# Two row stores moved from SyncE's DMA queue to GpSimd's, one pace point and one convolution slot moved later, in a fused convolution and gated feed-forward kernel

## The chip, the cores and the metric

The kernel runs on one core of one Trainium2 chip. The metric is the device time of one execution in microseconds; several executions are taken and their median is given. A separate execution is recorded by the hardware profiler, and every time of a single instruction or transfer below comes from that one. The engines are called as the profile calls them: PE is TensorE's matrix multiply and PEld its weight load, DVE is VectorE, ACT is ScalarE, POOL is GpSimd, and SP is SyncE, which here only issues DMAs. SP and POOL each have a DMA queue of their own; both feed the same 16 DMA engines.

## The reference

A depthwise convolution of seven taps (weights put through a softmax, the same for all 24 channels of a head) is followed by a feed-forward layer without a nonlinearity: two products, their elementwise product, and two more products.

```python
w = softmax(weight, axis=-1)                        # 8 heads x 7 taps
out[b, s, h, g] = sum_k w[h, k] * x_pad[b, s + k, h, g]   # x: 8 x 3904 x 192
x = out.reshape(31232, 192)
a = x @ w1                                          # 192 x 1024
b = x @ w2                                          # 192 x 1024
h = a * b @ w3                                      # (a * b) @ w3, 1024 x 1024
return h @ w_out                                    # 1024 x 192, float32
```

## The kernel before

**Tiling.** The tokens are cut into two streams of 15616 (NS = 2), which sit beside each other in the two halves of the partitions. A stream is cut into windows of 58 tokens, and these into 11 blocks, SIZES = 10, 8, 10, 8, then six of 36 and one of 20. A block is what is loaded, convolved and stored at a time. The feed-forward works in rounds of 512 tokens of each stream (31 rounds, taken in groups of four).

**One block's way.** `load_x` (line 98) loads a block's windows of x with DMAs of POOL's queue, which also turn float32 into bfloat16. `conv` (line 262) multiplies each head's windows with a band matrix on PE; the result is copied from PSUM into a `convo` tile by ACT or DVE (line 295). Then it has to be transposed to have channels on the partitions. Blocks 0, 1 and 2 are transposed by PE (`pe_transposes`, line 335). Block 3 onward, and the end of block 2 that round 3 needs, goes through DRAM: `store` (line 300) writes convo to the DRAM tile `rows` with DMAs of SP, and `transposes` (line 343) reads it back with three transposing DMAs of SP for a round, into the ring xT of four rounds. `send` (line 479) issues a round's three transposes as soon as its rows have been stored.

**A round.** `first_product` (line 361) makes both first products, eight steps `ft` of twelve matmuls, ACT copying one result and DVE multiplying it with the other into abT. A round takes 96 matmuls. A dictionary `between` names what is put behind which step: convolutions and PE transposes of the next blocks. `second_product` (line 388) multiplies abT of one stream of one round with W_sb, 32 matmuls, and stores the result; in the first group by POOL, later by SP.

**w3.** W_sb is w3 times w_out, made once. `load_w3` (line 424) copies w3 as bfloat16 to the DRAM tile `w3rows` by two DMAs of POOL, and SP reads it back transposed into w3T with 16 transposing DMAs (`w3_transposes`, line 428): eight for the first 512 rows of w3, eight for the others. `w3_product` (line 433) makes one of eight pieces of W_sb with eight matmuls. Pieces 0 to 3 read what the first eight transposes brought, pieces 4 to 7 the second eight, all eight of them for each piece.

**The order of the work.** The program is scheduled by hand: each engine runs its instructions in the order in which the code issues them and waits only where data or buffers make it. The prologue runs rounds 0 to 3 of first products (lines 484 to 503), with blocks 1 to 3 convolved in between; then the eight w3 products (line 517); then three heads of block 4 (`conv_heads`, line 509, with `slots` 0 to 2 of three, three and two heads, line 515); then the first group's eight second products, with the other heads of block 4 and all of block 5 between them at the places that `at` names (line 534). Behind the last heads of block 4, `conv_heads` stores the part of it that round 4 needs, sends round 4's transposes, and stores the rest; rounds 5 to 7 are sent by the call at line 543.

SP's order around the change is: the first five w3 transposes; six stores, two for the end of block 2 and four for block 3 (lines 494 and 495); the other three w3 transposes of the first half (line 496); round 3's three xT transposes (line 497); the second half's eight w3 transposes (line 498). POOL's order is: the loads of x of blocks 0 to 3 and of the weights; line 500, a copy of two numbers into the tile `pace`, which waits for the ninth w3 transpose since it reads what that one writes; then the ten loads of blocks 4 and 5, which stand behind it; then the zeroing of the padding rows of block 4 (`zero`, line 505), and the eight stores of second products.

Of the kernel before, what the change touches and what calls it, by code (L numbers as in the profile page):

```python
# [16 lines left out]
def kernel(  # L17
# [10 lines left out]
    nc = tc.nc  # L28
# [4 lines left out]
    DFF = moe_w1.shape[1]  # L33
    JT = DFF // 128
# [6 lines left out]
    GROUP = 4  # L41
# [5 lines left out]
    NWIN = (B // NS) * WB  # L47
    LAST = S - (WB - 1) * ST
# [7 lines left out]
    def tok(i):  # L56
        return (i // WB) * S + (i % WB) * ST
# [26 lines left out]
    rows = dram.tile([TS, NP * NS * Q], BF16, name="rows")  # L84
# [51 lines left out]
    pace = const.tile([1, 2], BF16)  # L136
# [31 lines left out]
    for p0 in (0, Q):  # L168
        nc.gpsimd.affine_select(
            out=diag[p0:p0 + Q], in_=ones[p0:p0 + Q].to_broadcast([Q, Q + PAD]),  # L170
# [3 lines left out]
    for r in range(NS):  # L174
        nc.gpsimd.dma_start(out=xb0[Q * r + PAD:Q * r + Q, 0, :],
                            in_=x_rows[r * TS:r * TS + ST, :])
# [13 lines left out]
    def warm(n, t=None):  # L190
# [16 lines left out]
        out=wall, in0=wall, in1=wmax.unsqueeze(2).to_broadcast([1, H, K]), op=ALU.subtract)  # L207
# [6 lines left out]
        out=wrow, in0=wall, in1=wsum.unsqueeze(2).to_broadcast([1, H, K]), op=ALU.mult)  # L214
# [47 lines left out]
    def conv(b, h0, nh, evict=None):  # L262
        n = SIZES[b] // 2
        if h0 == 0:
            convo_of[b] = work.tile([128, n, NP, NS, Q], BF16, tag="convo", bufs=2, name="convo")
        convo = convo_of[b]
        p, cps = banks()
        wd = nh * G

        def view(ps, r):  # L270
            return cps[ps, r, 0:n * wd].rearrange("p (w g) -> p w g", g=wd)

        for j in range(nh):
            h = h0 + j
            for c in range(2):
                xb, w0 = xb_of[b][c]
                for r in range(NS):
                    nc.tensor.matmul(  # L278
                        view(slice(Q * c, Q * c + Q), r)[:, :, j * G:(j + 1) * G],
                        band_of(h, r),  # L280
                        xb[Q * r:Q * r + Q, w0:w0 + n, h * G:(h + 1) * G],
                        start=True, stop=True)
        src = cps[:, :, 0:n * wd].rearrange("p r (w g) -> p r w g", g=wd)
        o, moves = 0, []
        for k, c0, m in segments(h0 * G, wd):
            moves.append((convo[:, :, k, :, c0:c0 + m].rearrange("p w r g -> p r w g"),
                          src[:, :, :, o:o + m]))
            o += m
        if h0 + nh == H:
            del xb_of[b]  # L290
        if evict == ():
            return p, moves
        for e, (dst, part) in enumerate(moves):
            f = evict or [nc.scalar.copy]
            f[e % len(f)](out=dst, in_=part)  # L295
        drained(p)

    stored, sent = [0], [GROUP - 1]

    def store(b, first=0, last=NWIN):  # L300
        n = SIZES[b] // 2
        last = min(last, FIRST[b] + 2 * n)
        stored[0] = tok(last) if last < NWIN else TS
        convo = convo_of[b]
        for c in range(2):
            i0 = FIRST[b] + c * n
            w, end = max(0, first - i0), min(n, last - i0)
            while w < end:
                left = WB - 1 - (i0 + w) % WB
                m = min(end - w, max(1, left))  # L310
                src = convo[Q * c:Q * c + ST, w:w + m].rearrange("s w k r g -> s w (k r g)")
                j0 = tok(i0 + w)
                if left == 0:
                    nc.sync.dma_start(out=rows[j0:j0 + LAST, :], in_=src[0:LAST, 0, :])
                else:
                    dst = rows[j0:j0 + ST * m, :].rearrange("(w s) c -> s w c", s=ST)
                    for s0, s1 in ((0, 48), (48, ST)):
                        nc.sync.dma_start(out=dst[s0:s1], in_=src[s0:s1])
                w += m

    def pe_transpose(b, k):
# [39 lines left out]
    def first_product(R, between=None):  # L361
        N = width(R)
        ab = work.tile([128, JT, NS, CH], BF16, tag="abT", bufs=GROUP, name="abT")
        abT_of[R] = ab
        r0 = (R * CH) % RING
        for ft in range(JT):
            pq = []
            for i in range(2):
                q, p = banks()
                pq.append((q, p))  # L370
                for k in range(NP):
                    for r in range(NS):
                        rs = slice(Q * r, Q * r + Q)
                        nc.tensor.matmul(  # L374
                            p[:, r, 0:N], wd[i][rs, k, ft * 128:(ft + 1) * 128],
                            xT[k][rs, r0:r0 + N],
                            start=(k == 0), stop=(k == NP - 1))
            (qa, pa), (qb, pb) = pq
            asb = work.tile([128, NS, CH], BF16, tag="asb", bufs=3, name="asb")
            nc.scalar.copy(out=asb[:, :, 0:N], in_=pa[:, :, 0:N])  # L380
            nc.vector.tensor_tensor(out=ab[:, ft, :, 0:N], in0=asb[:, :, 0:N],  # L381
                                    in1=pb[:, :, 0:N], op=ALU.mult)
            drained(qa)
            drained(qb)
            if between and ft in between:
                between[ft]()
# [34 lines left out]
    w3T = const.tile([128, JT, DFF], BF16)  # L421
# [6 lines left out]
    def w3_transposes(j, gts):  # L428
        for gt in gts:
            nc.sync.dma_start_transpose(  # L430
                out=w3T[:, gt, j:j + CH], in_=w3rows[j:j + CH, gt * 128:(gt + 1) * 128])

    def w3_product(jt):
        p, wps = banks()
        for gt in range(JT):
            nc.tensor.matmul(wps[:, 0, 0:D], w3T[:, gt, jt * 128:(jt + 1) * 128],  # L436
                             wo_b[:, gt, :], start=(gt == 0), stop=(gt == JT - 1))
        nc.scalar.copy(out=W_sb[:, jt, :], in_=wps[:, 0, 0:D])  # L438
        drained(p)


    V, A, P = nc.vector.tensor_copy, nc.scalar.copy, nc.gpsimd.tensor_copy
# [11 lines left out]
    for h, f in ((0, V), (2, A), (4, V), (6, A)):  # L454
        p, moves = conv(0, h, 2, ())
# [9 lines left out]
            copy_w(part, i, f)  # L465
    load_w3()
    nc.gpsimd.dma_start(out=wo_b, in_=wor)
    w3_transposes(0, range(5))

    def seq(*fs):  # L470
        def run():
            for f, *a in fs:
                f(*a)
        return run

    def need(R):
        return next(i for i in range(NWIN) if tok(i) >= (R + 1) * CH)

    def send(last):
        while sent[0] <= min(last, NR - 1) and min((sent[0] + 1) * CH, TS) <= stored[0]:  # L480
            transposes(sent[0])
            sent[0] += 1
# [6 lines left out]
        0: seq((conv, 2, 0, 4)),  # L489
        1: seq((conv, 2, 4, 4, (V,))),  # L490
        3: seq((conv, 3, 0, 4)),
        4: seq((conv, 3, 4, 4, (V,))),
        6: seq((pe_transposes, 2))})
    store(2, need(GROUP - 2) - 1)
    store(3)
    w3_transposes(0, range(5, JT))
    send(GROUP - 1)
    w3_transposes(CH, range(JT))
    first_product(2)
    P(out=pace, in_=w3T[0:1, 0, DFF - 2:DFF])  # L500
    load_x(4)
    load_x(5)
    first_product(3)
# [1 line left out]
    def zero(b):  # L505
        for xb, r, w in zero_rows.pop(b, []):
            nc.gpsimd.memset(xb[Q * r:Q * r + PAD, w, :], 0.0)  # L507

    def conv_heads(b, heads, f=(nc.vector.tensor_copy,), first=None):
        for j, h in enumerate(heads):  # L510
            conv(b, h, 1, (f[j % len(f)],))
        if heads[-1] == H - 1:
            store(b) if first is None else (store(b, last=first), send(NR), store(b, first))

    slots = (range(0, 3), range(3, 6), range(6, H))
    zero(4)
    for jt in range(JT):
        w3_product(jt)
    conv_heads(4, slots[0], (V, A))

    groups = [list(range(R, min(R + GROUP, NR))) for R in range(0, NR, GROUP)]
    assert groups[-1][-1] == NR - 1
    for p, rounds in enumerate(groups):
        b = PROLOGUE_BLOCKS + p
        order = rounds[-1:] + rounds[:-1] if rounds[-1] == NR - 1 else rounds
        for j, R in enumerate(order if p else ()):
            first_product(R)
            send(R + GROUP)
            if j < 2 and b < NB:
                P(out=pace, in_=abT_of[R][0:1, JT - 1, 1, 0:2])  # L530
                load_x(b, (j,))
        if b < NB:
            zero(b)
        at = {1: [(b, slots[0])], 3: [(b, slots[1])], 5: [(b, slots[2])]}
        if p == 0:
            at = {0: [(4, slots[1], (V, A))], 1: [(4, slots[2], (V, A), need(GROUP))],
                  3: at[1], 5: at[3], 6: at[5]}
        for i, (R, r) in enumerate((R, r) for R in rounds for r in range(NS)):
            second_product(R, r, R == NR - 1 and r == 1, nc.sync if p else nc.gpsimd)
            for c in at.get(i, ()) if b < NB else ():  # L540
                conv_heads(*c)
            if p == 0 and i == 1:
                send(2 * GROUP - 1)
    assert sent[0] == NR

# [29 lines left out]
```

## Time and profile before

| | |
|---|---|
| median of 3 runs | 527.39 us (526.74 to 527.83) |
| the profiled execution's own time | 527.34 us |
| its span, from the first instruction to the last | 525.6 us |
| PE busy | 514.5 us (98% of the span) |
| DVE, ACT, POOL busy | 360.7, 322.4, 55.4 us |
| mean granted TensorE clock | 0.996 of full speed |

The profiled execution's time is 1.7 us above its span and within 0.05 us of the median. A busy PE means here that some matmul is in flight; at 98% of the span, time can be gained only where PE stands idle, or runs at a lower clock, and time is lost by whatever makes PE wait. The order in time of the prologue on PE is: round 2 from 38.4 us, round 3 from 48.8 us, w3 products from 59.2 us, block 4's first heads from 69.8 us, second products up to 95.7 us, then round 4. From 95.7 us on the program repeats itself, group by group.

Two kinds of record are used below beside the instructions: each DMA issue has a start and an end on the engine that issues it, and each transfer counts a semaphore up when its parts have landed. The last count of a transfer is called its landing.

### The profile page before, as it was taken

To read this page: it belongs to the slowest core of one execution; us is meant where nothing else is said; L and a number is where in the kernel's file an instruction comes from. 1 tells how busy PE (TensorE), PEld (TensorE's weight loads), DVE (VectorE), ACT (ScalarE), POOL (GpSimd) and SP (SyncE) were. 2 spreads that over 40 slices of the span, in tenths; PEclk is the share of its full clock that TensorE was granted. 3 is DMA by queue.
4 is the path that set the end of the run, shared out by engine and by line. 5 is a ranking of instruction groups with operands and counts; after the bars stand their busy time and mean duration, and the time that the engine had idled before them with its cause. 6 is when DMAs were issued, how large, how long until landed. Compare 5 with 4: busy or idle time off the path is not lost.

```text
span 525.6 us, 12773 instructions
## 1 busy us (share of the span) xinstructions
PE 514.5 (98%) x5452; PEld 341.5 (65%) x5452; DVE 360.7 (69%) x350; ACT 322.4 (61%) x405; POOL 55.4 (11%) x93
## 2 busy tenths in 40 slices
PE   7999799999999999999999999999999999999997
PEld 4545579555795557955579555895558945599567
DVE  6779634799656996469963799637994289921880
ACT  5877543677536775367743777437774377734762
POOL 8402312112000110002100020000300000000000
PEclk9999989999999999999999999999999999999999
DMA  9995998899847893478834787357743632024004
GB/s 127 204 164 99 160 175 211 191 149 183 140 141 182 113 114 90 129 176 120 109 91 138 170 120 101 92 149 167 90 64 102 165 94 41 17 91 151 2 1 151
DMA packets 135613, 65.39 MB, mean 124 GB/s; under 512 B 91944, under 2 KB 134852, under 8 KB 135492
## 3 DMA queue, kind: packets, MB, share of 16 engines
q1 hardware_dynamic: 96610, 44.90, 37.9%
q0 software_dynamic: 38800, 19.58, 28.6%
q8 instruction: 42, 0.69, 0.6%
q14 instruction: 15, 0.12, 0.1%
q10 hardware_dynamic: 146, 0.10, 0.1%
HBM read 33.25 MB, written 36.92 MB: 133 GB/s over the span
## 4 chain that ended last, share of the span: by engine, by line
PE 90%; DMA 3%; SPq 2%; ACT 2%; DVE 1%; issue 1%; POOL 0%; POOLq 0%; ACTq 0%
PE pairs L374 55%; PE pairs L400 31%; PE pairs L278 3%; DMA w3T<-w3rows 2%; SPq L430 2%; ACT asb L380 1%; DVE abT L381 1%; DMA xb<-in_x_dram 1%; PE pairs L436 1%; DVE convo L295 0%; POOL xb L165 0%; PE pairs L327 0%; ACT xT L339 0%; ACT convo L295 0%; DVE convo L445 0%
## 5 line engine op out<-in xcount | busy, mean ns | idle before, releaser
L381 DVE TENSOR_TENSOR abT<-asb,pairs 128x1024 bf16<-128x1024 bf16 (+1 forms) x248 | 298.3, 1204 | 73.5 <-ACT asb L380 36.4
L374 PE MATMUL pairs<-xT,wd 64*128 64x512 bf16 (+1 forms) x2976 | 320.3, 373 | 1.2 <-DVE convo L295 0.3
L380 ACT CAST asb<-pairs 128x1024 bf16<-128x1024 f32 (+1 forms) x248 | 247.6, 998 | 69.9 <-PE pairs L374 69.4
L374 PEld LDWEIGHTS <-wd 64*128 64x128 bf16 x2976 | 163.4, 94 | 152.5 <-issue 3.9
L400 PEld LDWEIGHTS <-abT 128*128 128x128 bf16 x1952 | 159.6, 98 | 9.9 <-issue 9.9
L400 PE MATMUL pairs<-W_sb,abT 128*128 128x192 bf16 x1952 | 165.9, 246 | 0.0
L405 ACT COPY osb<-pairs 128x384 f32<-128x384 f32 x122 | 58.3, 478 | 115.9 <-PE pairs L400 115.9
L295 DVE CAST convo<-pairs 128x864 bf16<-128x864 f32 (+6 forms) x71 | 53.0, 803 | 72.8 <-PE pairs L278 67.9
L112 POOL DMA_DIRECT2D xb<-in_x_dram x40 | 30.9, 792 | 7.7 <-DMA xb<-in_x_dram 4.0
L530 POOL COPY pace<-abT 1x2 bf16<-1x2 bf16 x10 | 1.7, 174 | 241.1 <-DVE abT L381 241.1
L278 PE MATMUL pairs<-xb,Aband 64*64 64x432 bf16 (+3 forms) x352 | 17.0, 300 | 1.0 <-DMA xb<-in_x_dram 1.0
L278 PEld LDWEIGHTS <-Aband 64*64 64x64 bf16 x352 | 6.7, 107 | 8.2 <-issue 7.4
L436 PE MATMUL pairs<-wo_b,w3T 128*128 128x192 bf16 x64 | 7.0, 276 | 3.6 <-DMA w3T<-w3rows 3.6
L436 PEld LDWEIGHTS <-w3T 128*128 128x128 bf16 x64 | 6.2, 110 | 4.5 <-DMA w3T<-w3rows 4.0
L412 POOL DMA_DIRECT2D out_dram<-osb x8 | 6.1, 758 | 23.8 <-ACT osb L405 23.8
L405 DVE COPY osb<-pairs 128x192 f32<-128x192 f32 x1 | 0.4, 359 | 11.1 <-PE pairs L400 11.1
L438 ACT CAST W_sb<-pairs 128x192 bf16<-128x192 f32 x8 | 2.6, 319 | 7.9 <-PE pairs L436 7.9
L295 ACT CAST convo<-pairs 128x512 bf16<-128x512 f32 (+4 forms) x11 | 6.2, 605 | 1.1 <-PE pairs L278 1.0
L195 PE MATMUL pairs<-zeros 128*128 128x512 bf16 x8 | 3.7, 596 | 1.3 <-DVE zeros L145 1.3
L507 POOL MEMSET xb<- 6x192 bf16 x6 | 1.5, 250 | 22.5 <-DMA xb<-in_x_dram 22.4
L162 POOL DMA_DIRECT2D wd<-in_moe_w_dram x6 | 3.8, 641 | 0.0
L327 PE MATMUL pairs<-identw,convo 128*128 128x128 bf16 x42 | 3.1, 219 | 0.6 <-DVE convo L445 0.6
(51 smaller groups left out, 38.1 us busy)
## 6 DMA issues: line engine op xcount, KB each, us to landing
out_dram<-osb SPq DMA_DIRECT2D x52, 384.0 KB
xb<-in_x_dram POOLq DMA_DIRECT2D x18, 432.0 KB, 7.6
rows<-convo SPq DMA_DIRECT2D x8, 648.0 KB
out_dram<-osb POOLq DMA_DIRECT2D x8, 384.0 KB, 4.2
w3rows<-in_moe_w_dram POOLq DMA_DIRECT2D x2, 1024.0 KB, 10.8
xb<-in_x_dram POOLq DMA_DIRECT2D x6, 240.0 KB, 6.5
xT<-rows SPq DMA_TRANSPOSE x84
rows<-convo SPq DMA_DIRECT2D x4, 324.0 KB
```

What stands on the lines that cost most here:

```text
L112: nc.gpsimd.dma_start(out=xb[Q * r:Q * r + Q, w:w + m, :], in_=x_spans(r, i, m))
L162: nc.gpsimd.dma_start(out=wd[i][0:Q, :, cs], in_=w_rows[i][:, :, cs])
L278: nc.tensor.matmul(view(slice(Q * c, Q * c + Q), r)[:, :, j * G:(j + 1) * G], band_of(h, r), xb[Q * r:Q * r + Q, w0:w0 + n, h * G:(h + 1) ...
L295: f[e % len(f)](out=dst, in_=part)
L374: nc.tensor.matmul(p[:, r, 0:N], wd[i][rs, k, ft * 128:(ft + 1) * 128], xT[k][rs, r0:r0 + N], start=(k == 0), stop=(k == NP - 1))
L380: nc.scalar.copy(out=asb[:, :, 0:N], in_=pa[:, :, 0:N])
L381: nc.vector.tensor_tensor(out=ab[:, ft, :, 0:N], in0=asb[:, :, 0:N], in1=pb[:, :, 0:N], op=ALU.mult)
L400: nc.tensor.matmul(ops[:, (g - g0) * D:(g - g0) * D + D], ab[:, jt, r, g * 128:(g + 1) * 128], W_sb[:, jt, :], start=(jt == 0), stop=(jt = ...
L405: f(out=osb[:, g0:g0 + per, :].rearrange("p g d -> p (g d)"), in_=ops[:, 0:per * D])
L412: queue.dma_start(out=out[t0:t0 + ng * 128, :].rearrange("(g p) d -> p g d", p=128), in_=osb)
L430: nc.sync.dma_start_transpose(out=w3T[:, gt, j:j + CH], in_=w3rows[j:j + CH, gt * 128:(gt + 1) * 128])
L436: nc.tensor.matmul(wps[:, 0, 0:D], w3T[:, gt, jt * 128:(jt + 1) * 128], wo_b[:, gt, :], start=(gt == 0), stop=(gt == JT - 1))
```

## The change

The six stores of blocks 2 and 3 are issued by POOL's queue instead of SP's, so that SP issues all eight w3 transposes of the first half in a row. The pace copy reads what the twelfth w3 transpose writes, instead of the ninth, so block 4's and 5's loads start behind that one. The last four heads of block 3 are convolved behind step 5 of round 1 instead of step 4. Block 4's three parts are convolved behind the first, second and third second product, instead of before the first, behind the first and behind the second; block 5's first part moves from behind the fourth to behind the fifth, and rounds 5 to 7 are sent one second product later.

```diff
-    def store(b, first=0, last=NWIN):
+    def store(b, first=0, last=NWIN, queue=nc.sync):
...
-                    nc.sync.dma_start(out=rows[j0:j0 + LAST, :], in_=src[0:LAST, 0, :])
+                    queue.dma_start(out=rows[j0:j0 + LAST, :], in_=src[0:LAST, 0, :])
...
-                        nc.sync.dma_start(out=dst[s0:s1], in_=src[s0:s1])
+                        queue.dma_start(out=dst[s0:s1], in_=src[s0:s1])
...
-    w3_transposes(0, range(5))
+    w3_transposes(0, range(JT))
...
         3: seq((conv, 3, 0, 4)),
-        4: seq((conv, 3, 4, 4, (V,))),
+        5: seq((conv, 3, 4, 4, (V,))),
         6: seq((pe_transposes, 2))})
-    store(2, need(GROUP - 2) - 1)
-    store(3)
-    w3_transposes(0, range(5, JT))
+    store(2, need(GROUP - 2) - 1, queue=nc.gpsimd)
+    store(3, queue=nc.gpsimd)
     send(GROUP - 1)
     w3_transposes(CH, range(JT))
     first_product(2)
-    P(out=pace, in_=w3T[0:1, 0, DFF - 2:DFF])
+    P(out=pace, in_=w3T[0:1, JT // 2 - 1, DFF - 2:DFF])
     load_x(4)
     load_x(5)
     first_product(3)
...
     for jt in range(JT):
         w3_product(jt)
-    conv_heads(4, slots[0], (V, A))
...
         if p == 0:
-            at = {0: [(4, slots[1], (V, A))], 1: [(4, slots[2], (V, A), need(GROUP))],
-                  3: at[1], 5: at[3], 6: at[5]}
+            at = {0: [(4, slots[0], (V, A))], 1: [(4, slots[1], (V, A))],
+                  2: [(4, slots[2], (V, A), need(GROUP))], 4: at[1], 5: at[3], 6: at[5]}
...
-            if p == 0 and i == 1:
+            if p == 0 and i == 2:
                 send(2 * GROUP - 1)
```

## The prediction

> **What bounds the kernel now.** I read the page first (PE busy 98%, so only PE's gaps matter), then PE's waits between 36 and 110 us, where the change lies, then the stages by windows, then the chain of waits, and last the order of SP's and POOL's DMA issues. PE's waits have one line:
>
> ```profile
> PE pairs L436 <- DMA w3T<-w3rows: 3.6, 2, 2.2
> ```
>
> The w3 products wait 3.6 us, in two waits, for w3's transposes. The windows show that this isn't the whole price (columns: PE, PEld, DVE, ACT, POOL busy, granted clock, DMA share, GB/s):
>
> ```profile
> 59.24:62.55 3.31, 3.31 (x40) 3.08 (x38) 1.65 (x2) 1.75 (x5) 0.86 (x1) 1.00 1.92 150
> 62.55:66.41 3.86, 0.26 (x2) 0.10 (x2) 0.00 (x0) 0.00 (x0) 0.00 (x0) 1.00 1.23 149
> 67.23:70.64 3.41, 3.41 (x30) 2.52 (x27) 0.09 (x1) 0.96 (x3) 0.17 (x1) 0.50 1.60 192
> ```
>
> For 3.41 us behind the wait PE runs at half clock. The chain of waits shows what these stages cost in order (start, us, what):
>
> ```profile
> 55.76 10.60 DMA w3T<-w3rows
> ...
> 66.41 3.44 PE pairs L436 x25
> 69.85 1.07 PE pairs L278 x11
> 70.93 2.75 PE pairs L400 x32
> 73.67 0.67 PE pairs L278 x12
> ```
>
> The last w3 transpose takes 10.6 us. Why so long is seen in the issues of SP and POOL:
>
> ```profile
> 26.10 7.40 SPq L430 DMA_TRANSPOSE w3T<-w3rows  x5
> 33.63 3.33 SPq L318 DMA_DIRECT2D rows<-convo  x6
> 37.17 3.82 SPq L430 DMA_TRANSPOSE w3T<-w3rows  x3
> 41.23 4.71 SPq L347 DMA_TRANSPOSE xT<-rows  x3
> 45.99 12.16 SPq L430 DMA_TRANSPOSE w3T<-w3rows  x8
> ```
>
> ```profile
> 48.83 7.07 POOL L112 DMA_DIRECT2D xb<-in_x_dram  x9
> 59.87 0.86 POOL L112 DMA_DIRECT2D xb<-in_x_dram  x1 [3.97 <-DMA xb<-in_x_dram]
> 66.77 0.63 POOL L507 MEMSET xb<- 6x192 bf16 x2 [6.04 <-DMA xb<-in_x_dram]
> ```
>
> The ninth and tenth transposes land 2.65 and 2.6 us after their issues start (48.64 and 49.9 us). From about 50.7 us the loads of x move data too, and the next six land at 54.3, 57.7, 59.7, 61.5, 64.7 and 66.3: 2.4 us apart instead of 1.3. The two streams share the DMA engines, and x starts as soon as the ninth transpose has landed.
>
> **The change, part by part.**
>
> *Stores to POOL.* SP loses six issues (3.33 us). All eight transposes of the first half end at about 33.5 + 3 x 1.26 = 37.3 us, but what follows, round 3's xT, waits for the stores' landing. POOL has nothing else between 19.4 and 48.7 us. Block 3's last heads move one step of round 1 later: on DVE they follow the multiply of step 5, so their copies end at about 36.5 us instead of 35.1. POOL then issues four stores at 0.6 to 0.8 us each (its x loads take 0.67 to 0.93), the last from about 39 us. Before shows no store of rows from POOL. Lower bound of its landing: 3.35 us after the issue (the second products' stores, 83.78 to 87.13). Upper bound: 9.3 us (the second x load, 49.69 to 58.99). Nearest are POOL's own stores on a queue not saturated:
>
> ```profile
> out_dram<-osb POOLq DMA_DIRECT2D x8, 384.0 KB, 4.2
> ```
>
> These stores are smaller, so I take 3.5 us: landed at 42.5, xT's issues from there, 1.3 us after before's 41.23. Its third one is issued 2.5 us later and lands 2.65 us behind that, at 47.7 (48.7 if one issue takes 2.2 us, as one of before's did). Round 3 needs it 0.4 us after its start, at 49.2: nothing is lost, and 1.5 us is the cover. With the upper bound it lands at 53.5 and PE waits 4.3 us. So this edit alone gains nothing: the second half of w3 starts at 46.3 to 47.4 us, not earlier than 45.99.
>
> The Trainium skill speaks against this edit: DMA: Bandwidth & Descriptors, section "Issuing engine by pattern", gives plain stores to SyncE and calls its path generally faster. By the first-byte latencies of its section "Specifications" (about 1 us on GpSimd's path, 0.6 on SyncE's) it would cost 0.4 us of the cover, and the sum stays as it is. No run here yet shows a row store from POOL.
>
> *The pace.* The twelfth transpose starts three issues behind the ninth, at 46.8 + 3 x 1.26 = 50.6, and lands at 53.2 us; x starts at 53.4 instead of 48.83. Its data comes about 2 us later, at 55.4, when two transposes at most are left. Slowed to 2.4 to 2.7 us each, the last lands at 60 to 62 us. Its first reader stands at 59.24 + 4 x 0.69 + 0.6 = 62.6 us (0.087 us a matmul, 38 in 3.31). So w3's wait goes, and with it the half clock. If x came as early as before, the wait would stay.
>
> *x of block 4.* Before it lands at 67.1 us, 18.3 after its start. That fits 2 us to the first data, 9.8 us for its four units of 1152 rows (block 5's three units that follow w3 land 2.45 us apart), and 6 us for 3000 of w3's packets at the 500 packets a microsecond that the records show. Now about 1000 of these packets are left in its way, 2 us: it lands at 53.4 + 2 + 9.8 + 2 = 67.2, and POOL's zeroing is over at 67.9. Its bounds: 64.7 (started at 52.9, no w3 packet in the way), which PE would not notice, and 71.7 if it takes 18.3 us as before. I take 67.2, since the same sum gives before 48.83 + 17.8 = 66.6 where 67.1 was measured.
>
> *Block 4 one second product later.* PE now runs 64 w3 matmuls in 5.6 us without a break, then at once the first second product, 2.75 us. Its last matmuls need W_sb's last piece, whose copy takes 0.32 us; I charge 0.3 (0 to 0.5). PE wants x at 59.24 + 5.6 + 0.3 + 2.75 = 67.9 us, about when it is there. I charge 0.3 us for a short wait and 0.67 for the heads at full clock: 68.9 us. Before, the same work (w3, first heads, first second product) ended at 73.67. That is 4.8 us.
>
> *Downstream.* Between block 4's last heads and round 4 there is now one second product fewer (2.75 us). Before, SP needs 25.6 us from the copy of these heads (78.5) to the landing of round 5's third xT (104.1): the first stores, round 4's xT, seven more stores that take 10 us beside the second products' stores, then xT. Round 5 asks for it at 95.68 + 10.39 + 0.45 = 106.5, so 2.4 us are spare. In the new order PE leaves these heads at 75.6, their copy ends at 76.5, and xT lands at 102.1; round 5 asks at 75.6 + 15.3 + 10.39 + 0.45 = 101.7. I charge 0.4 us (0 to 2). Round 4's own xT has 2.5 us to spare, round 6's more. Block 5's heads, 3.05 us of DVE a part, now come in three neighbouring gaps 3.4 us apart, which covers them; if it didn't, PE would wait for a PSUM bank, at most some 0.3 us a part. Step 5's later heads delay DVE's xT copy of round 2 from 37.75 to about 38.2 us, just ahead of the round's start at 38.4: 0, up to 0.5.
>
> Sum: 4.8 - 0.4 - 0.2 (half of that last bound, rounded) = 4.2 us off the profiled execution's 527.34, 523.1 us; the median is 0.05 us away from it.
>
> **The rivals.**
>
> *The wait moves from w3 to x.* If the loads take 18.3 us as before, x is there at 71.7, the heads start at 72.2, and PE idles 4.3 us. Before, the clock was halved behind the stretch 63.81 to 67.23 us, in which PE had been busy 1.1 of 3.4 us; here such a stretch would come again, and cost half of some 1.8 us: the heads end at about 73.8, no gain, 527.4 us. For it: 18.3 is the only measured time of this load. Against: less of w3 is in its way. Half as late, the heads start at 70.0 and end, with half of that clock loss, at 71.1: 525.4. The Trainium skill, TensorE: Matmul & The Clock Gate, Part 1 (the HAM clock gate), halves the clock only after an idle window of about 3.4 us; by it the half-late case keeps full clock, but this trace's window, a third busy, was followed by half clock all the same.
>
> *POOL's stores land late (slower).* At 9.3 us they land at 48.3, xT's third at 53.5, round 3 stalls 4.3 us, a halved clock adds up to 1.7, everything on SP and x come 5.8 us later: the heads end at 68.9 + 5.8 to 75.2, against 73.67. That is 1.5 us lost, 528.9 us. It decides from about 7.9 us of landing on (3.5 and the 4.4 us of gain, since x and w3 shift with it). For it: POOL's loads took 6 to 10 us beside w3's transposes. Against: at 37 to 42 us the DMA engines are half idle.
>
> *Round 5's xT is late.* If the stores of block 4 collide with block 5's x, the 25.6 us become 29: 3.4 us back, 526.5.
>
> *The change doesn't do what it says:* w3's last transpose, issued at 55.6 since its series starts no earlier, takes 10.6 us again and lands at 66.2. Then w3 ends where it did, 69.85, the heads at 73.6 to 74.0: 527.5. Against: before's was issued when x had moved data for 5 us, this one when x has just begun.
>
> **How the numbers follow.** Forecast 0.60, own range 521.6 to 524.8 (the bounds of bubble, zeroing, downstream). Wait moved to x 0.15 (half as late 0.08, whole 0.07); late stores, slower, 0.13; round 5, 0.07; w3 late anyhow, 0.05. Some 0.2% (1.05 us) is what a measurement can tell from no change. Faster: the forecast and the half-late x, 0.68; same: whole delay of x, round 5, w3 late, 0.19; slower 0.13. The range goes from 521.6 to 527.4; it leaves out the late stores and the late w3, 0.18.
>
> **What would show it.** Right: no wait of L436 on w3T, no half clock in the middle, POOL's x loads from about 53 us, heads of block 4 at about 68 us, round 4 at about 91 us. Wrong: PE waiting at the start of round 3 or at L278 for xb, or L374 waiting for xT at round 5. The prediction falls if POOL's row stores land more than 6 us after their issue, or if x's loads need over 16 us.

## The result, and the profile after

The changed kernel takes 524.24 us (median of 9 runs, 523.65 to 526.05), the kernel before beside it 527.09 us (9 runs, 524.60 to 529.01). The ratio is 0.9948, with a 95% interval from 0.9927 to 0.9969: 2.85 us faster between the medians. The profiled execution has a span of 521.9 us, 3.7 less than before's 525.6, and a granted clock of 1.0.

PE's waits between 14 and 140 us in the changed kernel (engine and line, waiting for what: us in total, times, longest):

```profile
PE pairs L436 <- DMA w3T<-w3rows: 1.9, 1, 1.9
PE pairs L327 <- DVE convo L295: 0.4, 1, 0.4
PE pairs L374 <- DVE convo L295: 0.3, 1, 0.3
```

The wait for w3's transposes has shrunk from 3.6 to 1.9 us; it has not gone. No wait for x, and none for an xT, has come in its place. The chain of waits shows where the time was won:

```profile
55.11 9.25 DMA w3T<-w3rows
64.36 0.05 issue
64.41 2.24 PE pairs L436 x25
66.65 2.64 PE pairs L400 x32
69.29 0.67 PE pairs L278 x12
...
92.07 18.02 PE pairs L374 x165
```

The last 25 w3 matmuls take 2.24 us, where before's last 25 took 3.44, from 67.23 us on at half clock. The first second product and block 4's first heads are done at 69.96 us instead of 73.67 (3.7 us), and round 4 starts at 92.07 instead of 95.68 (3.6 us); later stages keep the difference. Of the 3.7 us, w3's earlier last transpose gives 2.0 (66.41 against 64.41) and PE's kept clock 1.7 (7.26 us from there to the end of both stages in the kernel before, 5.55 here). The windows give the clock (PE, PEld, DVE, ACT, POOL busy, granted clock, DMA share, GB/s):

```profile
62.53:64.41 1.88, 0.00 (x1) 0.00 (x1) 0.00 (x0) 0.00 (x0) 0.00 (x0) 1.00 1.33 161
64.41:66.65 2.24, 2.24 (x28) 2.24 (x28) 0.00 (x0) 0.95 (x3) 0.85 (x1) 1.00 1.60 191
```

SP's and POOL's issues:

```profile
26.22 11.84 SPq L430 DMA_TRANSPOSE w3T<-w3rows  x8
41.42 4.52 SPq L347 DMA_TRANSPOSE xT<-rows  x3
46.04 10.56 SPq L430 DMA_TRANSPOSE w3T<-w3rows  x8
```

```profile
36.91 2.31 POOL L318 DMA_DIRECT2D rows<-convo  x4 [5.28 <-ACT xT L339]
52.56 0.17 POOL L499 COPY pace<-w3T 1x2 bf16<-1x2 bf16 x1 [13.34 <-DMA w3T<-w3rows]
52.79 6.22 POOL L112 DMA_DIRECT2D xb<-in_x_dram  x8
...
68.77 0.25 POOL L506 MEMSET xb<- 6x192 bf16 x1 [0.22 <-DMA xb<-in_x_dram]
```

w3's second half starts at 46.04 us, where before's started at 45.99: the stores' new queue has moved it by nothing. SP now idles from 38.05 to 41.42 us, waiting for the stores. x starts 4.0 us later than before, and its padding rows are zeroed at 69.02 us, 0.27 us ahead of its heads.

The medians differ by 2.85 us and the traces by 3.7, because the changed kernel's profiled execution is the fastest of its nine, 0.6 us under their median, and before's lies 0.25 us above its own. Much of the scatter between executions is PE's clock. Each run lists its mean clock: seven of the changed kernel's nine runs had no half clock but for the end (1.0, 523.65 to 524.81 us), two had one window of it (0.997 and 0.996, 526.05 and 525.79). Of 25 runs of the kernel before that stood beside the first experiments, two had none (525.18 and 525.27), 17 had one (0.996 or 0.997, 525.90 to 528.48) and six had two (0.992 or 0.993, 528.09 to 529.26). Among executions without half clock the two kernels differ by less: 524.1 us is the mean of the changed kernel's seven, 525.2 that of before's two, and in a later session on one chip it is 524.8 against 525.2, five executions each. So much of the gain is that the changed kernel meets the half clock less often: in 7 of its 19 executions in these sessions, against 49 of before's 56. The mean doesn't tell where a window lies. In before's profile it lies behind the wait for w3, where the change works; in three profiles below it lies between 10 and 15 us, at the program's start, and moves everything behind it by 2.0 to 2.5 us. The experiments are therefore compared, beside their times, by the stretch from PE's first matmul behind block 2's transposes to the start of round 4, read from the chain of waits: before 95.68 - 37.12 = 58.6 us, changed 92.07 - 37.08 = 55.0.

### The profile page after: what moved, and what is told of

Its sections match the earlier page's. It is cut to its first block, busy times and chain, and to the rows that moved or that the text cites. A ratio compares the mean times of both kernels' runs of the same rounds, so it can differ in the third digit from the quotient of the medians.

```text
span 521.9 us, 12776 instructions
## 1 busy us (share of the span) xinstructions
PE 513.1 (98%) x5452; PEld 340.3 (65%) x5452; DVE 360.1 (69%) x350; ACT 322.3 (62%) x405; POOL 59.0 (11%) x99
## 4 chain that ended last, share of the span: by engine, by line
PE 91%; DMA 3%; SPq 2%; ACT 2%; DVE 1%; issue 1%; POOL 0%; POOLq 0%; ACTq 0%
PE pairs L374 56%; PE pairs L400 31%; PE pairs L278 2%; DMA w3T<-w3rows 2%; SPq L430 2%; ACT asb L380 1%; DVE abT L381 1%; DMA xb<-in_x_dram 1%; PE pairs L436 0%; DVE convo L295 0%; PE pairs L327 0%; POOL xb L165 0%; DVE convo L445 0%; ACT xT L445 0%; SPq L347 0%
## 5 line engine op out<-in xcount | busy, mean ns | idle before, releaser
L436 PE MATMUL pairs<-wo_b,w3T 128*128 128x192 bf16 x64 | 5.6, 246 | 1.9 <-DMA w3T<-w3rows 1.9
L436 PEld LDWEIGHTS <-w3T 128*128 128x128 bf16 x64 | 5.2, 98 | 2.5 <-DMA w3T<-w3rows 2.1
L318 POOL DMA_DIRECT2D rows<-convo x6 | 3.5, 590 | 16.3 <-DVE convo L295 11.1
(52 smaller groups left out, 42.5 us busy)
```

## The experiments

All are edits of the changed kernel. The ratios are to the kernel before, run beside them.

**Stores back on SP.** Only the queue, and with it the place of the first half's last three transposes, is undone.

```diff
-    w3_transposes(0, range(JT))
+    w3_transposes(0, range(5))
...
-    store(2, need(GROUP - 2) - 1, queue=nc.gpsimd)
-    store(3, queue=nc.gpsimd)
+    store(2, need(GROUP - 2) - 1)
+    store(3)
+    w3_transposes(0, range(5, JT))
```

> Of the change only the stores go back to SP (and the last three transposes of w3's first half behind them). Theory (the gain comes from the pace and from block 4's later place; the stores' queue gives nothing): round 3's xT and w3's second half move by 0 to 1 us, since SP now waits for block 3's copies at 36.4 us and then issues six stores and three transposes; PE's wait for w3T 1.9 to 2.9 us, round 4 from 92 to 93 us, span 522 to 523. Rival (SP's free queue is what gives the gain): the wait for w3T goes back to 3.6 us with the half clock, round 4 from 95 us on, span 525.

Measured: ratio 0.9944 (0.9925 to 0.9964), span 522.3, stretch 55.3 us. PE's waits and SP's issues in this run:

```profile
PE pairs L436 <- DMA w3T<-w3rows: 2.0, 2, 1.4
```

```profile
33.80 4.22 SPq L318 DMA_DIRECT2D rows<-convo  x6
38.06 3.73 SPq L430 DMA_TRANSPOSE w3T<-w3rows  x3
42.04 4.36 SPq L347 DMA_TRANSPOSE xT<-rows  x3
46.45 10.94 SPq L430 DMA_TRANSPOSE w3T<-w3rows  x8
```

With the stores on SP the second half starts 0.4 us later, and the kernel is as fast. The moved stores are not where the gain comes from.

**Pace back on the ninth transpose.**

```diff
-    P(out=pace, in_=w3T[0:1, JT // 2 - 1, DFF - 2:DFF])
+    P(out=pace, in_=w3T[0:1, 0, DFF - 2:DFF])
```

> Of the change only the pace goes back to the ninth transpose. Theory (x in w3's way makes the wait): x starts at 48.8 us, w3's last transpose lands at about 66 us, PE waits 3.5 us and runs at half clock behind it, the first second product ends at about 72.7 and the first heads at 73.4, round 4 from 95.5 us, span 525.4. Rival (the stores' queue gives the gain): the wait stays at 1.9 us, round 4 from 92 us, span 522.

Measured: ratio 1.0013 (0.9995 to 1.0030), span 525.2, stretch 58.0 us. All ten runs show at least one window of half clock. PE's waits, and the window of half clock:

```profile
PE pairs L436 <- DMA w3T<-w3rows: 3.2, 2, 1.7
```

```profile
65.91:69.33 3.42, 3.26 (x21) 3.08 (x22) 0.00 (x0) 0.95 (x3) 0.50 (x2) 0.50 1.60 191
```

Without the later pace nothing is left of the gain, though the stores and block 4 are where the change put them.

**Block 4 back at its old place.** With it go back block 5's first part and the call that sends rounds 5 to 7.

```diff
     for jt in range(JT):
         w3_product(jt)
+    conv_heads(4, slots[0], (V, A))
...
-            at = {0: [(4, slots[0], (V, A))], 1: [(4, slots[1], (V, A))],
-                  2: [(4, slots[2], (V, A), need(GROUP))], 4: at[1], 5: at[3], 6: at[5]}
+            at = {0: [(4, slots[1], (V, A))], 1: [(4, slots[2], (V, A), need(GROUP))],
+                  3: at[1], 5: at[3], 6: at[5]}
...
-            if p == 0 and i == 2:
+            if p == 0 and i == 1:
```

> Of the change only block 4's and 5's places (and the place of the send) go back. Theory (x is zeroed at 69.0 us in the changed kernel, 0.3 us ahead of its heads, so their later place hides it): PE leaves w3 at 66.6 us and waits 2.4 us for x at L278; first heads and first second product end at 72.5 instead of 70.0, with a halved clock up to 1.7 us later; round 4 from 94.6 to 96.3 us, span 524.4 to 526.1. Rival (w3's wait was all that mattered, the place gives nothing): round 4 from 92 us, span 522.

Measured: ratio 1.0007 (0.9989 to 1.0026), span 526.7, stretch 59.4 us. PE's waits:

```profile
PE pairs L278 <- POOL xb L506: 2.0, 2, 1.8
PE pairs L436 <- DMA w3T<-w3rows: 2.0, 1, 2.0
```

Both waits stand now, and a half-clock window from 71.1 us follows. Seven of ten runs had one half-clock window somewhere (528.03 to 529.34 us), three had none (525.67 to 526.66). So the later pace and the later heads are one edit in two parts: either alone gives nothing.

**Pace on the last transpose.** x starts when w3 is through, which measures both transfers without the other.

```diff
-    P(out=pace, in_=w3T[0:1, JT // 2 - 1, DFF - 2:DFF])
+    P(out=pace, in_=w3T[0:1, JT - 1, DFF - 2:DFF])
```

> The pace waits for the sixteenth transpose instead of the twelfth. Theory (x slows w3's transposes from 2.6 to 9 us): the sixteenth, issued at about 55 us, lands at 57.8; PE has no wait for w3T; x starts at 57.9 and is there at about 70, so PE waits some 2.9 us for x at the heads, which end at 71.1 instead of 70.0; round 4 from 93.2 to 94.2 us, span 523 to 524. Rival (the last transposes are slow of themselves, or by other traffic): PE still waits for w3T 1 us or more, and for x on top, span 525 or more.

Measured: ratio 1.0030 (1.0008 to 1.0053), span 525.1, stretch 57.8 us. The sixteenth transpose is issued at 55.05 us and lands at 57.79, 2.7 us later instead of 9.25 (from the chain of waits):

```profile
55.05 2.74 DMA w3T<-w3rows
...
58.08 0.46 POOL xb L112
```

x starts at 58.08 and lands at 70.60, in 12.5 us. PE has no wait for w3T but one for x:

```profile
PE pairs L278 <- POOL xb L506: 2.6, 1, 2.6
```

```profile
67.20:70.61 3.41, 0.80 (x8) 0.38 (x6) 0.00 (x0) 0.48 (x1) 0.80 (x2) 1.00 1.60 190
70.61:74.02 3.41, 3.41 (x23) 2.28 (x23) 2.08 (x3) 0.88 (x1) 1.05 (x2) 0.50 1.60 192
```

The wait was foreseen, the half clock behind it was not priced in full: 55.0 and the expected 1.1 make 56.1, and the other 1.7 us are half of that window. All ten runs had at least one window of half clock. x in w3's way is what makes w3 late.

**Step 4 again for block 3's last heads.**

```diff
-        5: seq((conv, 3, 4, 4, (V,))),
+        4: seq((conv, 3, 4, 4, (V,))),
```

> Of the change only the place of block 3's last heads goes back, to step 4 of round 1; its stores stay on POOL. Theory (SP waits from 38.1 to 41.4 us for the stores' landing, and the later copy at 36.3 us makes that wait): the copy ends at 35.2, the stores land at 39.6, xT and w3's second half start 1.7 us earlier, w3's last transpose lands at about 62.7; PE's wait for w3T is 0.2 to 0.5 us, x is zeroed at 67.3; round 4 from 90.4 us, span 520.3. Rival (the stores land with w3's transposes, not with the copy): xT from 41 us on as now, span 522.

Measured: ratio 0.9960 (0.9935 to 0.9985), span 524.2, stretch 57.3 us, of which 1.7 are half of a half-clock window. The theory fell: the stores are issued 1.2 us earlier, but xT still starts when it did (SP's issues):

```profile
26.59 12.68 SPq L430 DMA_TRANSPOSE w3T<-w3rows  x8
41.49 4.32 SPq L347 DMA_TRANSPOSE xT<-rows  x3
```

The first half's transposes end 1.2 us later (39.27 instead of 38.06), and the stores, issued from 35.68 to 37.99, land at 40.3 to 41.4: the two streams take the time from each other. This run's wait for w3T was 2.7 us, and the half clock followed; the changed kernel has the latter in two of nine runs, this one in five of ten, which is no clear difference.

**Two transposes in SP's gap.** The 3.4 us in which SP waits for the stores are used for the first two transposes of the second half. The pace goes to the fourteenth; a second run leaves it on the twelfth, a third takes the thirteenth. The diff is the first run's; in the others gt is 3 and 4 in place of 5.

```diff
     store(3, queue=nc.gpsimd)
+    w3_transposes(CH, range(2))
     send(GROUP - 1)
-    w3_transposes(CH, range(JT))
+    w3_transposes(CH, range(2, JT))
     first_product(2)
-    P(out=pace, in_=w3T[0:1, JT // 2 - 1, DFF - 2:DFF])
+    P(out=pace, in_=w3T[0:1, 5, DFF - 2:DFF])
```

> The changed kernel with the first two transposes of w3's second half ahead of round 3's xT, in the 3.4 us in which SP waits for POOL's stores, and the pace on the fourteenth transpose, which is then issued when the twelfth was. Theory (w3's wait comes from x taking the DMA engines while four transposes are still open): the last transpose is issued at 52.5 us and lands by 58; no wait for w3T; x starts at 52.8 us as before this edit, has two transposes fewer in its way and is zeroed at 67.0; heads of block 4 from 67.4 us, round 4 from 90.2 us, span 520, and no half clock in any run. Rival (the DMA engines' whole work between 46 and 68 us is the bound, whatever its order): x is no earlier than 69, PE waits for it instead, span 522 or more. Round 3's xT would show it if the two transposes cost it its cover (a wait of L374 at 48.8 us).

> As the run with two transposes in SP's gap, but the pace stays on the twelfth transpose, so x starts 2.5 us earlier and has four transposes in its way again. Theory: w3's last transpose lands at 61.8 us, 0.6 ahead of its reader; x is zeroed at 66.5; round 4 from 90.2 us as in the other run, since neither is waited for; if x's start holds the transposes up longer (3 us at its start, 3.2 a piece after), PE waits up to 1 us for w3T and round 4 starts at up to 91.2. Rival (DMA work is the bound in any order): span 522.

> The changed kernel once more, beside the others on one chip: span 522, round 4 from 92.1 us, a ratio of 0.9948 within 0.002. Where the 1.9 us wait falls across PE's clock windows decides whether the half clock comes, so some runs are about 1.7 us longer and show a mean clock of 0.997.

> Two transposes in SP's gap as before, pace on the thirteenth, between the two runs that had it on the twelfth (w3 waited 0.7 us) and the fourteenth (no wait for w3, the heads 0.5 us late). Expected if both waits follow x's start one for one: neither of the two, from round 2's start to round 4's 53.1 to 53.5 us (53.8 and 53.5 in those two, 55.0 in the changed kernel), span 520, ratio 0.9915 to 0.993. If x's start holds the transposes up by a fixed time whenever it comes, a wait of 0.3 to 1 us stays and nothing is gained on them.

| | ratio (95%) | median, us | stretch, us | waits of PE in it |
|---|---|---|---|---|
| pace 14th | 0.9928 (0.9907 to 0.9949) | 523.07 | 53.5 | none over 0.4; heads 0.5 slower |
| pace 12th | 0.9923 (0.9902 to 0.9944) | 523.05 | 53.8 | w3T 0.7 |
| pace 13th | 0.9919 (0.9891 to 0.9947) | 523.18 | 54.2 | xT of round 3 0.6; heads 0.5 slower |
| changed kernel again | 0.9965 (0.9942 to 0.9987) | 525.91 | 54.9 | w3T 1.8 |

The first, the second and the last ran on one chip. There the two in the gap are 2.8 us faster than the changed kernel by their medians, 1.1 to 1.4 us by the stretch. A part of the rest goes with the half clock, which two of ten runs of each of the two have, and five of ten of the changed kernel: among the runs without it the difference is 1.8 to 1.9 us (522.8 and 522.9 against 524.8 on average). The remaining half a microsecond is not explained. The profile of the changed kernel's second run has it at the start: PE's round 2 begins 2.5 us later, and the stretch is the same within 0.1 us. In the thirteenth's profile the last store landed 4.6 us after its issue (2.7 in the changed kernel, 3.4 and 3.9 in the other two with transposes in the gap), and round 3's third xT at 50.1 us, instead of 47.6. The two extra transposes thus cost xT its cover in one profile of three, though SP's order is the same in all. All three versions beat the kernel before, and the two on the changed kernel's chip beat that one too. The expected 53.1 came in none of them: the gain was 0.8 to 1.5 us where 1.9 was expected, since for what w3 no longer waits, block 4's heads or round 3 wait 0.5 to 0.6 us, or w3 still does 0.7. The rival, that the DMA engines' work bounds the stage in any order, fits this remainder; no run tests it by itself.

**x's first load in halves.** In the changed kernel x's first data moves at 54.4 us, and from 54.8 until 58.0 the open transposes move next to nothing. Whether the size of x's first loads does this is tested by cutting block 4's first two loads.

```diff
-                    for r in range(NS):
-                        nc.gpsimd.dma_start(out=xb[Q * r:Q * r + Q, w:w + m, :],
-                                            in_=x_spans(r, i, m))
+                    cut = (0, 9, 18) if i == FIRST[4] else (0, m)
+                    for v0, v1 in zip(cut, cut[1:]):
+                        for r in range(NS):
+                            nc.gpsimd.dma_start(out=xb[Q * r:Q * r + Q, w + v0:w + v1, :],
+                                                in_=x_spans(r, i + v0, v1 - v0))
```

> The changed kernel with block 4's first two loads of 18 windows cut into four of 9; the same bytes. In the changed kernel the fourteenth to sixteenth transposes land 2 to 3 us late from the moment x's data starts, and x's first load moves meanwhile without them. Theory (the transposes are held until the first x load has gone through, and share evenly after): with halves the hold is some 1.2 us shorter, the sixteenth lands at about 63.2, PE's wait for w3T is 0.5 to 1 us; round 2 to round 4 about 54 us. Rival (the hold has nothing to do with the size of a load): the wait stays near 1.9 us, 55 us, and x may land later by the two more issues (1.4 us), so the heads could wait too.

> Both edits together: two transposes in SP's gap, pace on the twelfth, block 4's first two loads halved. In the run without the halves w3 still waited 0.7 us, since the open transposes stood still for 2.3 us when x's data began. Theory (the hold lasts as long as x's first load): it lasts 1.5 us or less, w3 doesn't wait, the heads wait 0 to 0.5 us; from round 2's start to round 4's 53.1 to 53.7 us (53.8 without the halves), span 519.8 to 520.4, ratio about 0.991. Rival (the hold has nothing to do with a load's size): w3 waits 0.7 us or more as before, 53.8 us or more.

Measured, alone: ratio 0.9965 (0.9945 to 0.9984), stretch 54.6 us; PE has no wait for w3T and 1.0 us for x. This run had the half clock at the start, as the changed kernel's second one; there the sixteenth transpose landed 5 us after PE began with w3, here 2.2 us. With the two in the gap: ratio 0.9928 (0.9903 to 0.9953), stretch 53.8 us. PE's wait in the first, and PE's order in the second (start, us, what):

```profile
PE pairs L280 <- POOL xb L508: 1.0, 2, 0.8
```

```profile
59.39 5.45 PE L438 MATMUL pairs<-wo_b,w3T 128*128 128x192 bf16 x64
64.68 2.80 PE L402 MATMUL pairs<-W_sb,abT 128*128 128x192 bf16 x32
67.42 1.58 PE L280 MATMUL pairs<-xb,Aband 64*64 64x432 bf16 x12
```

The 64 w3 matmuls run without a break, and the heads take 1.58 us instead of 0.74.

By the packets, counted in quarters of a microsecond, the transposes all but stand still (under 20 of their packets in a quarter) for some 3.5 us soon after x's first data in five profiles with whole loads, before and changed among them. In four others a first standstill of 2.0 to 3.0 us is followed by a second of 1.0 to 1.25, and with the pace on the fourteenth, where w3 is nearly through, there is one of 2.0. With halves the first lasts about 1.8 us and a second follows, of 1.4 us (halves alone) or 0.75 (with the two in the gap). So the first standstill is shorter with halves, as the theory has it, but the sum of both with the halves alone, 3.2 us, is no shorter than the 3.2 of the shortest pair with whole loads: the theory isn't settled. Why the transposes stand back, the trace doesn't say. For the time the halves gave nothing: w3's wait of 0.7 us went, and the heads' came.

## Why the prediction was right, and where it was off

The prediction gave 523.1 us with a range of 521.6 to 527.4, and faster; 524.24 lies in it. The predicted gain was 4.2 us, 2.85 came by the medians and 3.7 by the profiled spans. The direction and the two steps that carry it (x later, its reader later still) were right for the reason given. That no wait for w3T would be left was wrong. That the half clock stayed away from the profiled execution all the same was luck: nothing in the prediction says that a wait of 1.9 us would be short enough.

- *Stores to POOL gain nothing.* Right, shown by the run with the stores on SP. The stores landed at 41.36, 2.7 us after the last one's issue at 38.65 (predicted 3.5), xT started at 41.42 (42.5), its third landed at 47.6 (47.7): the cover was 1.5 us, as predicted. The rival of late stores is out. The Trainium skill's preference for SyncE in plain stores (DMA: Bandwidth & Descriptors, section "Issuing engine by pattern") did not show clearly in the landing: the last of the six stores took 3.2 us from its issue on SP in the kernel before, 2.6 on SP in the run with the stores there, and 2.7 on POOL. An issue costs POOL 0.6 us and SP 0.3 to 0.5.
- *The pace.* x started at 52.79 us (predicted 53.4). That it is what frees w3 is shown by the runs with the ninth and the last transpose.
- *w3's last transpose at 60 to 62 us.* This is the step that failed in size: it landed at 64.36, so that PE kept a wait of 1.9 us. I charged the two transposes in x's company 2.4 to 2.7 us each, the mean of before's, in which six share the standstill at x's start. Here only two to three are left to carry it. The records show two stretches that made it late: next to nothing moved for w3 from 54.8 to 58.0 us, and from about 61.5 all 16 DMA engines stood for some 1.2 us. The first goes with the begin of x's data, for a reason that stays open; so does the cause of the second.
- *The half clock goes with the wait.* In the profile it went, but not because the wait did: 1.9 us of waiting were left, and the window of 3.41 us that holds this wait whole, from 61.88 us, still had PE busy 45%. The wait of 2.7 us in the run with step 4 brought the half clock back. In two of the changed kernel's nine runs, and in five of ten later ones, there is a window of it, which may lie at w3 or at the start, where the change does nothing.
- *x zeroed at 67.9 us.* It was 69.02, 1.1 late: 1312 of w3's packets were still to come when x's data began, where the sum had 1000, and the sum had no pause of 1.2 us in it. This cost nothing more, because PE had lost its 1.9 us at w3: the heads started at 69.29. Had w3 been on time, PE would have waited for x. The runs with two in the gap show it: they win 0.8 to 1.5 of the 1.9 us.
- *The sum to block 4's heads.* 4.8 us were predicted, 73.67 - 69.96 = 3.7 measured. The 1.1 us between them are w3's wait, or x's lateness, whichever is taken away last.
- *Downstream 0.4 us.* Not needed: round 5's third xT landed at about 102.4, and PE asked for it at 92.07 + 10.39 + 0.45 = 102.9. The later step for block 3 gave a wait of 0.37 us on DVE ahead of block 2's transposes, inside a stretch that ended no later (37.08 against 37.12 us): 0.2 were charged.

Of the rivals, "the wait moves from w3 to x" is what the run with the last transpose does, with 2.6 us; the changed kernel is 0.27 us away from it. "The change doesn't do what it says" came half true: w3's last transpose took 9.25 us, nearly as long as before's 10.6, but was issued 0.65 us earlier and waited for by a PE that kept its clock. Of the signs that the prediction named for being right, x's loads from about 53 us came (52.79) and so did the missing half clock, in this profile; the wait of L436 stayed, and the heads and round 4 were 1.1 to 1.3 us later than the 68 and 91 named. One reading of the prediction was off without consequence: it gives POOL's loads beside w3's transposes 6 to 10 us, but of before's x loads the first two took 5.6 and 9.3 from issue to landing and the next two 12.9 and 15.1.

## What to carry to other kernels

Two transfers that share the DMA engines should be timed by who needs which first: delay the one that is needed later, and move its reader as far back as it is delayed; here either half alone gave nothing. After freeing a queue, look for where it stands idle now, and put the next needed transfer there: two transposes in SP's new gap of 3.4 us were worth 1.1 to 1.4 us, the stores' move by itself nothing. And price a wait of PE with the clock behind it: here each window of 3.41 us in which PE worked about a third of the time or less was followed by one at half clock, which costs another 1.7 us.

## What the runs showed of the hardware

- The half clock doesn't need an idle window. At w3 and block 4's heads, the windows of 3.41 us behind which it came had PE busy 12, 23, 32, 34 and 49% of the time (the last with many of the convolution's small 64x64 matmuls); behind windows of 45, 59 and more it didn't. At the program's start it came behind windows of 48, 51 and 53%, and not behind 59 and more. So the busy share alone doesn't decide it: the window with 45% kept the clock, those with 48 to 53% lost it, and what else counts is open. The grid of these windows lies elsewhere in each execution: the first window on record begins 4.5 to 7.7 us after the span's start in the thirteen profiles. Which executions of the changed kernel lose the clock at w3 is not shown: both of its profiles keep it there, one with the wait whole in one window and one with it split over two (80 and 69% busy). The Trainium skill, TensorE: Matmul & The Clock Gate, Part 1, asks for an idle window of about 3.4 us; here waits of 2.6 and 2.7 us, each in one piece, were enough.
- A transposing DMA of 512x128 lands 2.6 to 2.8 us after its issue starts (the changed kernel's ninth to thirteenth), and the next issue starts 1.30 us behind it, while x's loads don't move. When a load of POOL's queue begins beside it, the transposes all but stand still for 1.8 to 3.5 us before the two share about evenly (some 70 packets each in a quarter of a microsecond).
- Some 1.2 us long, around 61.5 to 62.8 us in the changed kernel, packets of both queues that normally take 0.02 to 0.05 us took up to 1.4 us, on all DMA engines at once. It shows in seven of the thirteen profiles (before, changed twice, stores on SP, pace on the ninth, heads early, step 4), those in which w3's transposes were still moving then, and not in the six in which they were through. In these seven, the queue that the profile calls instruction starts a packet of 16 KB some 0.7 to 1.3 us ahead of the pause; the other six have such a packet too, without the pause. Its cause was not tried.
